# Attention in front of a routed expert layer: exponentials of phi into PSUM, masks by TensorE, casts and subtractions on other engines, and a written-out order

## The chip, the cores and the metric

One core of one Trainium2 chip runs one program. The time is device microseconds for one execution; lower is better. Of three timed runs of the kernel before, the median is 904.42 us (904.2 to 906.09).

## The reference

Two stages. Attention takes q, k, v of 8 batches, 8 heads, 576 positions and 64 columns; each head gets causal softmax attention plus a linear memory read by phi(q), and the two are mixed by a gate:

```
scores = q k^T / 8, masked above the diagonal, minus their row maximum
local  = softmax(scores) v
phi(x) = where(x > 0, x, exp(x) - 1) + 1          # = max(x,0) + exp(-max(-x,0))
mem    = (phi(q) M_prev) / (phi(q) z_prev + 1e-6)
x      = g*mem + (1-g)*local,  g = sigmoid(beta)   # 4608 tokens x 512
```

Then a routed layer: logits `x @ w_gate` are sorted over all (token, expert) pairs, each token takes the best expert that still has room (576 per expert), and expert e gives `relu(x w1[e]) w2[e]`.

## The kernel before

Everything is float32 in and out; TensorE works on float16 pairs. A float32 tile is cast to a float16 high half, the remainder is subtracted out as a low half, and products are summed over high and low parts.

**Attention** runs in 16 units (a unit is one batch and four of its heads). Per unit: SP loads k, q, v and M; casts make the high halves (`kh`, `qh`, `vh`, and `ph` of phi), subtractions the low halves (`kl`, `ql`, `vl`, `pl`, line 1043 and 1154 on GpSimd); TensorE transposes them (line 1052) and copies out of PSUM give `kT`, `qT`, `pT`. phi is three steps: a relu on ScalarE (`phr`, line 1137), an exponential in place in SBUF on ScalarE (`phe`, line 1138), and max-plus-add on VectorE (`phs`, line 1139), each over 18x64 = 1152 columns.

A first pass finds each row's maximum (`MX`): TensorE writes 128x512 blocks of scores to a PSUM bank `pb`, and VectorE reduces them. Rows of a block on the diagonal need the causal mask; line 1067 adds it while reducing, with one custom instruction per row block (512, 384, 256 or 128 columns), each followed by a reading of its accumulator (`DVE_READ_ACCUMULATOR2_ANT`). The maximum goes back into a spare row of `qM`, so that the second pass of scores comes out of TensorE with it subtracted. ScalarE takes the exponential (line 1205 a float16 `ph`; lines 1209 and 1212 a float32 copy), and VectorE (line 1210, from PSUM) or GpSimd (line 1213) subtracts to a low half `pl`.

Each head's output is accumulated by TensorE in `avo`, two PSUM tiles used in turn (the parts AV1, AV2, AV3), and the memory's part in `avm`, one tile (AVm). VectorE then makes the denominators (N0: lines 1260 for `avo`, 1261 for `avm`), their reciprocal (N1, 1265), and scales both (N2, 1264); GpSimd adds the two (`nadd`, 1272), and a cast and a subtraction give `xs`, which goes to DRAM and, transposed, to the gate's logits. In one head of four VectorE adds instead (N2b, N3: line 1278).

**Order.** Each piece of work is a node with engines it may run on, costs, dependences and buffers from pools (`pb` 5, `av` 2, `am` 1, ...). `Sched.run` is a planner: it walks simulated time with those costs and the priorities and offsets of the table `PR` (`off`, `dl`, `pin` for the engine) and emits one list; each engine executes its share of that list in order, and waits between engines are semaphores that the tile layer derives from the tiles that instructions write and read. **The expert layer** (`moe_all`) has a planner run of its own.

Of the kernel before, what the change touches and what calls it, by code (L numbers as in the profile page):

```python
# [23 lines left out]
 'dl': {'0': {'AV': -2321.92,  # L24
              'MX': 1567.76,
              'N': -24421.58,
              'P2': -4357.96,
              'S': 101.14,
              'fin1': 22868.1,
              'fin2': 10356.86,  # L30
              'kb': 10286.06,
              'kh': -45730.44,
              'kl': 20174.46,
              'kt': -4701.95,
              'lk': -12408.59,
              'lm': -8436.44,
              'lq': -2541.36,
              'lv': -3.36,
              'maxrem': 3733.37,
              'mfin': 29276.67,  # L40
              'mfin2': -10538.29,
              'mfin3': 7506.77,
              'mh': -11209.39,
              'ml': -432.1,
              'mz': 12658.92,
              'nadd': -11907.02,
              'ncast': -7225.71,
              'nsub': -10647.97,
              'ph': -1228.79,
              'phe': -9589.46,  # L50
              'phr': 524.92,
              'phs': 2230.42,
              'pl': 4308.28,
              'proc24': 3267.06,
              'pt': 11255.13,
              'qh': -4155.4,
              'ql': 7002.13,
              'qmove': -223.83,
              'qt': 10808.21,
              'sj4': 22053.16,  # L60
              'vh': -293.15,
              'vl': -4289.79},
        '1': {'AV': -11630.65,
              'MX': 5085.57,
              'N': -6291.91,
              'P2': -3722.96,
              'S': 0.29,
              'fin1': 18360.27,
              'fin2': -6498.84,
              'kb': -13149.86,  # L70
              'kh': -9834.86,
              'kl': -14831.77,
              'kt': 2765.98,
              'lk': -26.17,
              'lm': -31.5,
              'lq': -62.5,
              'lv': 65.33,
              'maxrem': 241.19,
              'mfin': 827.99,
              'mfin2': 5904.98,  # L80
              'mfin3': 8067.82,
              'mh': -6693.41,
              'ml': -3921.85,
              'mz': 12321.27,
              'nadd': 28446.8,
              'ncast': -5424.62,
              'nsub': -11693.87,
              'ph': 492.03,
              'phe': 2716.39,
              'phr': -7873.98,  # L90
              'phs': -15036.85,
              'pl': 8602.27,
              'proc24': -8298.99,
              'pt': 9687.89,
              'qh': 27462.53,
              'ql': -726.83,
              'qmove': -2093.73,
              'qt': -7770.46,
              'sj4': 1.71,
              'vh': -3758.76,  # L100
              'vl': -4489.33},
        '10': {'AV': 2861.92,
               'MX': 0.01,
               'N': -4207.12,
               'P2': -7603.6,
               'S': -0.44,
               'fin1': -11796.22,
# [36 lines left out]
               'P2': -700.32,
               'S': 0.11,
               'fin1': -8124.01,
               'fin2': -3919.93,
               'kb': 9923.63,
               'kh': 12644.97,
               'kl': -13145.41,  # L150
               'kt': -4241.87,
               'lk': -6151.58,
               'lm': -7286.77,
               'lq': 7551.39,
               'lv': 7510.93,
               'maxrem': 2.79,
               'mfin': 22015.1,
               'mfin2': 6463.64,
               'mfin3': -7945.76,
               'mh': -9010.16,  # L160
               'ml': 7934.19,
               'mz': -3520.69,
               'nadd': 2187.16,
               'ncast': 12966.79,
               'nsub': -4987.87,
               'ph': 4067.79,
               'phe': 16439.48,
               'phr': -16517.7,
               'phs': 7862.4,
               'pl': 3996.54,  # L170
               'proc24': 2350.4,
               'pt': -0.15,
               'qh': 1067.34,
               'ql': 512.84,
               'qmove': -18712.55,
               'qt': -9981.91,
               'sj4': -4091.57,
               'vh': -11967.99,
               'vl': -5668.57},
        '12': {'AV': 13431.14,  # L180
               'MX': -0.34,
               'N': 6485.25,
               'P2': -2957.52,
               'S': 0.54,
               'fin1': -4378.18,
               'fin2': 23705.86,
               'kb': -1628.06,
               'kh': -4672.12,
               'kl': 9427.26,
               'kt': -3533.86,  # L190
               'lk': -3255.11,
               'lm': 3597.42,
               'lq': 2527.1,
               'lv': 5090.06,
               'maxrem': 0.14,
               'mfin': -7530.28,
               'mfin2': -24054.29,
               'mfin3': -4992.24,
               'mh': 2100.24,
               'ml': 10776.14,  # L200
               'mz': -6507.17,
# [542 lines left out]
class Sched:  # L744
# [18 lines left out]
    def run(self,tol=100,sem=170,same=110,t0=0.0,hwg=450,dlat=1300,dend=950,ph=2800.0,thr=3060,pel=60):  # L763
# [43 lines left out]
        while left:  # L807
            b=None
# [966 lines left out]
```

## Time and profile before

| | us |
|---|---|
| timed runs, median (lowest to highest) | 904.42 (904.2 to 906.09) |
| the profiled execution, its own time | 910.64 |
| its span, first to last instruction | 908.8 |
| attention, filling: 0 to 100 of the span | 100 |
| attention, steady: 100 to 425 | 325 |
| attention, last head, last logits, routing's preparation: 425 to 441 | 16 |
| routing and experts: 441 to 908.8 | 468 |

A row of an engine gives its busy time. For TensorE a record of a matmul lasts longer than the engine is taken by it (the next starts long before the record ends), so TensorE's share is an upper bound. On VectorE and ScalarE one record's last 0.08 to 0.1 us lie under the next record's start, so the cost of an instruction in a full queue is the distance between two starts.

### The profile page before, as it was taken

The page shows a single profiled execution, that of the slowest core. Times are in us where ns is not written, and L with a number is a line of the kernel's source. Part 1 is how long each engine was busy: PE and PEld are TensorE (multiplying, and loading weights), DVE is VectorE, ACT ScalarE, POOL GpSimd, SP SyncE. Part 2 cuts the span into 40 slices and gives each one's busy share as a digit, 9 for nine tenths or more (in the row PEclk, how much of TensorE's full clock was granted, in tenths as well). Part 3 has the DMA queues.
Part 4 walks back from the last instruction along what each step waited for, and adds up shares of the span by engine and source line. Part 5 has one row for each costly group of instructions (what it writes and reads, how often), then busy time and mean ns, then how long its engine had stood idle before and what let it go on. Part 6 is the DMA issues. An engine that isn't in the chain of part 4 may idle for free.

```text
span 908.8 us, 24389 instructions
## 1 busy us (share of the span) xinstructions
PE 803.3 (88%) x9240; PEld 526.2 (58%) x9240; DVE 670.7 (74%) x2507; ACT 580.7 (64%) x1027; POOL 543.7 (60%) x564
## 2 busy tenths in 40 slices
PE   3687998999999899999226999999999999999995
PEld 2475887777787688888115445454444444444442
DVE  8798898999999899997788878787867774111020
ACT  4767787887898888976226674848383846552120
POOL 5776886887898786866104492928174646852101
PEclk9999899999999999999557999999999999999998
DMA  5566777765757566334124455566463828940001
GB/s 127 117 142 132 166 155 156 165 149 127 161 130 168 120 139 136 86 71 92 48 93 146 164 144 195 143 213 148 167 168 124 226 89 208 248 150 18 35 13 41
DMA packets 231755, 120.86 MB, mean 133 GB/s; under 512 B 199509, under 2 KB 208725, under 8 KB 231637
## 3 DMA queue, kind: packets, MB, share of 16 engines
q1 hardware_dynamic: 225749, 100.42, 45.2%
q0 software_dynamic: 5888, 18.88, 6.7%
q8 instruction: 72, 1.18, 0.5%
q14 instruction: 46, 0.38, 0.1%
HBM read 72.40 MB, written 18.87 MB: 100 GB/s over the span
## 4 chain that ended last, share of the span: by engine, by line
PE 49%; DVE 22%; issue 12%; DMA 6%; POOL 5%; ACT 3%; SPq 2%; another core or an unknown queue 0%; POOLq 0%; DVEq 0%; ACTq 0%
PE py L1417 15%; PE ph L1417 15%; PE pb L892 7%; PE avo L892 5%; DVE pb L1067 4%; DVE scr L1658 2%; DVE xt L1264 2%; DMA xT<-xs 2%; PE pb L1052 2%; PE prem L1417 2%; DVE pl L1210 2%; SPq L959 1%; POOL h L1043 1%; PE pr L1417 1%; DMA qM<-qT 1%
## 5 line engine op out<-in xcount | busy, mean ns | idle before, releaser
L1574 POOL TENSOR_TENSOR wl<-wst,wh 128x1024 f16<-128x1024 f32 x62 | 131.3, 2140 | 80.8 <-ACT wh L1573 59.5
L1417 PE MATMUL ph<-xT,wh 128*128 128x512 f16 (+1 forms) x560 | 162.9, 364 | 2.8 <-DVE hl L1617 1.4
L1067 DVE CUSTOM_DVE_ANT_0 pb<-pb,maskF 128x128 f32<-128x128 f32 (+3 forms) x256 | 124.7, 497 | 7.4 <-PE pb L892 3.7
L892 PE MATMUL pb<-qT,kT 128*128 128x64 f16 (+3 forms) x576 | 106.1, 245 | 8.2 <-DVE mx L1067 1.8
L1636 POOL DMA_INDIRECT out_dram<-ys,idx x40 | 38.9, 973 | 119.1 <-ACT ys L1631 99.8
L1205 ACT ACTIVATE ph<-pb 128x512 f16<-128x512 f32 x144 | 86.0, 597 | 29.1 <-PE pb L892 23.0
L1617 DVE SCALAR_TENSOR_TENSOR hl<-ph,hh 128x512 f16<-128x512 f32 x64 | 44.0, 688 | 80.2 <-ACT hh L1616 77.2
L1417 PEld LDWEIGHTS <-wh 128*128 128x128 f16 x1072 | 68.4, 98 | 59.6 <-issue 3.5
L892 PE MATMUL pb<-qM,kB 128*128 128x64 f16 (+3 forms) x576 | 99.2, 244 | 1.7 <-DMA qM<-mr 1.7
L1417 PE MATMUL py<-wh,hh 128*128 128x512 f16 x256 | 97.0, 379 | 1.5 <-ACT hh L1616 1.1
L1417 PE MATMUL ph<-xT,wl 128*128 128x512 f16 (+1 forms) x280 | 97.7, 363 | 0.0
L1417 PE MATMUL py<-wl,hh 128*128 128x512 f16 x256 | 97.0, 379 | 0.0
L1417 PE MATMUL prem<-xT,wh 128*128 128x64 f16 x512 | 96.3, 193 | 0.0
L1658 DVE TENSOR_SCALAR_CACHE_REDUCE scr<-p_LwT,th 128x320 f16<-128x320 f32 x168 | 85.1, 543 | 2.7
L1616 ACT ACTIVATE hh<-ph 128x512 f16<-128x512 f32 x64 | 38.0, 593 | 76.2 <-PE ph L1417 55.5
L892 PE MATMUL pb<-kT,qM 128*128 128x512 f16 (+5 forms) x384 | 77.6, 314 | 8.8 <-DVE mx L1067 3.4
L1417 PEld LDWEIGHTS <-hh 128*128 128x128 f16 x512 | 47.3, 97 | 56.2 <-ACT hh L1616 1.3
L1656 ACT ACTIVATE scs<-p_LwT,th 128x320 f16<-128x320 f32 x84 | 47.0, 560 | 50.7 <-DVE th L1665 40.2
L892 PE MATMUL avo<-V,ph 128*128 128x65 f16 x1344 | 78.7, 194 | 0.0
L892 PE MATMUL avo<-V,pl 128*128 128x65 f16 x672 | 74.9, 196 | 0.0
L892 PEld LDWEIGHTS <-ph 128*128 128x128 f16 x1344 | 70.6, 98 | 5.1 <-issue 0.9
L1496 POOL DMA_INDIRECT xg<-xd,idx x40 | 38.6, 964 | 51.6 <-DVE sa L1517 35.0
(304 smaller groups left out, 2358.3 us busy)
## 6 DMA issues: line engine op xcount, KB each, us to landing
wst<-in_moe_w_dram SPq DMA_DIRECT2D x32, 1024.0 KB, 7.7
kf<-in_k_dram SPq DMA_DIRECT2D x64, 128.0 KB, 2.8
qf<-in_q_dram SPq DMA_DIRECT2D x64, 128.0 KB, 2.8
xd<-xs SPq DMA_DIRECT2D x16, 512.0 KB, 3.5
vf<-in_v_dram SPq DMA_DIRECT2D x48, 128.0 KB, 2.8
kB<-kT SPq DMA_DIRECT2D x15, 288.0 KB, 3.4
qM<-qT SPq DMA_DIRECT2D x15, 288.0 KB, 5.5
vF<-in_v_dram SPq DMA_DIRECT2D x16, 128.0 KB, 3.1
```

Source lines behind the costliest of these rows:

```text
L892: def MM(*a,**kw): mm(*a,skip_group_check=True,**kw)
L1052: for i in range(a,b_): nc.tensor.transpose(p[:,128*(i-a):128*(i-a)+128],g()[:,i],cst['idh'])
L1067: Q=lambda o,i,n: nc.vector.tensor_tensor_reduce(out=i,in0=i,in1=cst['maskF'][:,512-n:512],scale=1.0,scalar=-3e38,op0=ALU.add,op1=ALU.max, ...
L1205: c=SC.add('Eh',[('A',478)],lambda x,a=a: nc.scalar.activation(phs_[x.buf['ph']][:,0:512],pbb[a.buf['pb']],AF.Exp,scale=0.125),acq=('ph',) ...
L1417: def MM(*a,**kw): mm(*a,skip_group_check=True,**kw)
L1496: SC.add('gather',[('P',1250 if i<4 else 1200,'p',0,(1250,'n'))],lambda x: G_.indirect_dma_start(out=xg[0:r_,i],out_offset=None,in_=xd,in_ ...
L1574: SC.add('sp',[('P',2079)],lambda x,ws=ws,k=k,s=s: G_.tensor_sub(wl[:,k,s],ws(),wh[:,k,s]),r=[key+('h',)],w=[key+('l',)],after=[b],rel=rel ...
L1616: b=SC.add('hh',[('A',478)],lambda x,a0=a0,f=f: A_.activation(hh[:,f],phb[a0.buf['ph']],AF.Relu),w=[('hh',f)],after=[y],prio=pr('hh',n,pos ...
L1617: SC.add('hl',[('V',602)],lambda x,a0=a0,f=f: V_.scalar_tensor_tensor(hl[:,f],phb[a0.buf['ph']],0.0,hh[:,f],op0=ALU.max,op1=ALU.subtract), ...
L1636: SC.add('scat',[('P',1250 if i<4 else 1200,'p',0,(1250,'n'))],lambda x,e=e,i=i,r_=r_: G_.indirect_dma_start(out=outv[5*n+i],out_offset=ba ...
L1656: SC.add('sign',[('A',547)],lambda x,j=j,t_=t_,c_=c_: A_.activation(scs[j-KV],LwT,AF.Sign,bias=t_[:,4:5],accum_out=c_[:,j:j+1]),r=['LwT',( ...
L1658: V(462,lambda x,j=j,t_=t_,c_=c_: V_.tensor_scalar(scr[j],LwT,t_[:,j+1:j+2],0.0,op0=ALU.is_ge,op1=ALU.add,accum_out=c_[:,j:j+1]),r=['LwT', ...
```

## The change

Only attention is edited; `moe_all` stands as it was.

- phi's exponential goes to a PSUM bank of the pool `pb`, in pieces of 8, 8 and 2 tiles (512, 512, 128 columns) instead of in place in SBUF; `phs` reads it there.
- The masks of the smaller row blocks (384, 256, 128 columns) are added by TensorE, as one more 128x128 matmul of `identb` with `maskM` per block, and VectorE takes plain maxima (`TENSOR_REDUCE`), two blocks of 256 in one instruction. The 512-column block keeps the custom instruction.
- `avo` and `avm` become one tile `avb` of three banks (`avo` 0, `avm`, `avo` 1), so that N0 is one instruction for both denominators and, in three heads of four, N2 one of 640 columns.
- Beyond the first unit, low halves (`kl`, `ql`, `vl`, `pl`, `p4s`, `ml`, `nsub`) run on GpSimd alone; the high-half casts and the relu no longer have VectorE as a choice; copies of the memory (`mz`, `mh`, `mh2`) run on ScalarE alone.
- The planner is not run for attention: `Sched.given` takes a list of node numbers, of chosen engines and of buffers (`PR_ORDER`), which replaces the tables `dl`, `off` and `pin`.

```diff
-              'phe': -9589.46,
+ 'dl': {},
+ 'off': {},
+ 'pin': {},
+PR_ORDER = ('''
+5 24 3 21 26 4 22 25 1 23 2 27 28 31 0 32 41 29 43 42 30 45 6 44 47 245 46 49 239 57 111 51 48 241 50 59 238 114 53 115 440 61 52 58 116 242 63 9 60 112 243 62 10 65 8 64 67 7 70 240 66 14 69 68
...
+    def given(self,ids,alts,bufs):
+
+        al,bu=[iter(''.join(x.split())) for x in (alts,bufs)]; free={k:set(range(v)) for k,v in self.pools.items()}; out=[]
+        for i in map(int,ids.split()):
+            x=self.n[i]; a=x.alts[int(next(al)) if len(x.alts)>1 else 0]; x.eng=a[0]; x.var=a[2] if len(a)>2 else None
+            assert all(d.start is not None for d in x.deps)
+            for p in x.acq: x.buf[p]=int(next(bu)); free[p].remove(x.buf[p])
+            for p,o in x.rel: free[p].add(o.buf[p])
+            x.start=len(out); out.append(x)
...
-    avo=[ps.tile([128,512],F32,name=f'avo{i}') for i in range(2)]; avm=ps.tile([128,512],F32,name='avm')
+    avb=ps.tile([128,3,512],F32,name='avb'); avo=[avb[:,0],avb[:,2]]; avm=avb[:,1]
...
+            rq=MK(u)+[('qMz',u%3)]; mk=lambda o: MM(o,identb,maskM,start=False,stop=True)
...
-                        MM(p[:,0:384],qT[:,4*h+2],kq(h,3),start=True,stop=True)
-                        MM(p[:,384:512],qT[:,4*h],kq(h,1),start=True,stop=True)
-                    def f2(p,h=h): Q(mx[:,4*h+2:4*h+3],p[:,0:384],384); Q(mx[:,4*h:4*h+1],p[:,384:512],128)
+                        MM(p[:,0:384],qT[:,4*h+2],kq(h,3),start=True,stop=False); mk(p[:,256:384])
+                        MM(p[:,384:512],qT[:,4*h],kq(h,1),start=True,stop=False); mk(p[:,384:512])
+                    def f2(p,h=h): R(mx[:,4*h+2:4*h+3],p[:,0:384]); R(mx[:,4*h:4*h+1],p[:,384:512])
...
-                    for y in range(2): Q(mx[:,8*h2+4*y+1:8*h2+4*y+2],p[:,256*y:256*y+256],256)
+                def f2(p,h2=h2): R(mx[:,8*h2+1:8*h2+8:4],p.rearrange('p (a b) -> p a b',b=256))
...
-            SC.add('phe',[('A',Ac(n))],lambda x,a=a,b_=b_,UE=u%NE: nc.scalar.activation(ef[UE][:,a:b_],ef[UE][:,a:b_],AF.Exp,scale=-1.0),w=K('ef',u%NE,a,b_),prio=pr('phe',u))
+            for c0_ in range(a,b_,8):
+                c1_=min(c0_+8,b_); n=n64(c0_,c1_); pv=lambda x,n=n: pbb[x.buf['pb']][:,0:n].rearrange('p (t d) -> p t d',d=64)
+                y=SC.add('phe',[('A',75+.81*n)],lambda x,a=c0_,b_=c1_,UE=u%NE,pv=pv: nc.scalar.activation(pv(x),ef[UE][:,a:b_],AF.Exp,scale=-1.0),r=K('ef',u%NE,c0_,c1_),acq=('pb',),prio=pr('phe',u))
+                SC.add('phs',[('V',Vt(n))],lambda x,a=c0_,b_=c1_,U2=U2,UE=u%NE,pv=pv,y=y: nc.vector.scalar_tensor_tensor(ef[UE][:,a:b_],qf[U2][:,a:b_],0.0,pv(y),op0=ALU.max,op1=ALU.add),r=K('qf',U2,c0_,c1_),w=K('ef',u%NE,c0_,c1_),after=[y],rel=[('pb',y)],prio=pr('phs',u))
...
-        SC.add('mz',al('mz',u,a=97,v=75),lambda x,u=u,U2=U2: cp(x.var,mf[U2][:,:,64],zT[0:64,4*u:4*u+4]),r=['zT'],w=[('mf',U2,2)],prio=pr('mz',u))
+        SC.add('mz',al('mz',u,a=90),lambda x,u=u,U2=U2: cp(x.var,mf[U2][:,:,64],zT[0:64,4*u:4*u+4]),r=['zT'],w=[('mf',U2,2)],prio=pr('mz',u))
...
-                nc.vector.scalar_tensor_tensor(de[:,0:5],own(0,5)[:,:,64],1.0/256,eg(0,5),op0=ALU.mult,op1=ALU.add)
-                nc.vector.scalar_tensor_tensor(de[:,5:10],mem()[:,:,64],1.0/256,eg(5,10),op0=ALU.mult,op1=ALU.add)
+            def f(x): nc.vector.scalar_tensor_tensor(des[di],both()[:,:,:,64],1.0/256,eps[:,g,5*bo():5*bo()+10].rearrange('p (k i) -> p k i',i=5),op0=ALU.mult,op1=ALU.add)
...
-    order=SC.run(**P_.get('run',{}))
+    order=SC.run(PR_ORDER)
```

What each engine executes differs at two places that matter below.

VectorE before, in the maxima of one unit and the scaling of one head (`ISA pb,mx<-pb,maskF` is the custom maximum, `ISA mx` its reading, `xt` the scaled output N2):

```order
L1067 ISA pb_180,mx_162<-pb_180,maskF 128x384
L1067 ISA mx_162 128x1
L1067 ISA pb_180,mx_162<-pb_180,maskF 128x128
L1067 ISA mx_162 128x1
L1264 TENSOR_TENSOR xt_170<-avo_104,de_166 128x320
L1264 TENSOR_TENSOR xt_170<-avm,de_166 128x320
```

VectorE now, at such a place (`de` are the denominators, N0 and N1; `ef` is phi's sum, read from a `pb` bank):

```order
L678 SCALAR_TENSOR_TENSOR de_165<-avb,eps 128x10
L682 RECIPROCAL de_165<-de_165 128x10
L480 TENSOR_REDUCE mx_161<-pb_179 128x1 x2
L687 TENSOR_TENSOR xt_167<-avb,de_165 128x640
L480 TENSOR_REDUCE mx_161<-pb_177 128x2
L625 TENSOR_TENSOR pl_140<-pb_178,ph_133 128x512
L480 TENSOR_REDUCE mx_161<-pb_179 128x1 x2
L554 SCALAR_TENSOR_TENSOR ef_111<-qf_108,pb_177 128x512
```

The pairs of custom maxima with their readings became plain reductions without a reading, N0 and N2 one instruction each, and phi's sum three shorter ones.

TensorE before, where the memory's part of one head (`avm`) ends and the next head's accumulation (`avo`) starts; what an instruction waits for stands in brackets:

```order
L892 MATMUL avm<-ml_131,pT_125 128x65
L892 LDWEIGHTS pT_125
L892 MATMUL avm<-mh_129,pT_125 128x65
L892 LDWEIGHTS pT_125
L892 MATMUL avm<-ml_131,pT_125 128x65
L892 MATMUL avo_105<-vF_159,pf_150 128x65 x2
L892 MATMUL avo_105<-vF_159,pf_151 128x65
L892 LDWEIGHTS qM_99
```

TensorE now, inside one head's accumulation (the end of AV1 and the start of AV2, both into bank 0 of `avb`):

```order
L306 MATMUL avb<-V_103,ph_131 128x65
L306 LDWEIGHTS pl_138 [waits Pool_49]
L306 MATMUL avb<-V_103,pl_138 128x65
L306 LDWEIGHTS ph_134
L306 MATMUL avb<-V_103,ph_134 128x65 [waits DVE_49]
L306 LDWEIGHTS ph_134
L306 MATMUL avb<-V_103,ph_134 128x65
```

And VectorE now, the instructions of the head before that this accumulation waits for, one for each of AV1, AV2 and AV3 (N2, N2b, N3; they read bank 1, bank 2 and bank 2):

```order
L682 RECIPROCAL de_165<-de_165 128x10
L681 TENSOR_TENSOR xt_166<-avb,de_165 128x320
L681 TENSOR_TENSOR avb<-avb,de_165 128x5x64
L695 TENSOR_TENSOR xt_166<-avb,xt_166 128x320
L348 CAST xs_170<-xt_166 128x5x64
```

Matmuls into these banks that wait for VectorE were 22 in the whole program and are 111. Followed back to the instruction that each waits for, 109 of them wait for one that reads other banks than the matmul writes: the waits go by the tile, and the three banks are one tile now.

## Rows read from the trace of the kernel before

**Rows 1.** Stretches: us, busy us of PE, PEld, DVE, ACT, POOL, clock, DMA:
```profile
0.00:100.00 100.00, 69.45 (x920) 52.57 (x920) 83.81 (x259) 65.01 (x110) 67.59 (x143) 0.95 0.63 138
100.00:425.00 325.00, 307.76 (x5354) 258.71 (x5351) 305.87 (x998) 273.24 (x497) 260.11 (x272) 0.99 0.60 133
425.00:441.00 16.00, 9.66 (x168) 8.76 (x164) 8.76 (x42) 4.68 (x10) 7.06 (x9) 0.78 0.45 117
441.00:909.00 468.00, 416.44 (x2810) 206.11 (x2810) 272.30 (x1210) 237.75 (x412) 208.92 (x143) 0.94 0.45 133
```
**Rows 2.** Who waited for whom, 100 to 425: total us, times, longest:
```profile
ACT ph L1205 <- PE pb L892: 22.5, 22, 3.6
POOL xt L1272 <- DVE xt L1264: 10.2, 6, 4.1
```
**Rows 3.** The same view, 0 to 441, TensorE on VectorE's scaling:
```profile
PE avm L892 <- DVE xt L1264: 1.3, 1, 1.3
```
**Rows 4.** Timeline, TensorE: start us, length us, instruction:
```profile
251.23 0.19 PE L892 MATMUL avm<-ml,pT 128*128 128x65 f16 x1
251.26 0.38 PE L892 MATMUL pb<-qT,kT 128*128 128x512 f16 x1
251.48 0.38 PE L892 MATMUL pb<-qM,kB 128*128 128x512 f16 x1
251.69 0.22 PE L892 MATMUL pb<-maskT,identb 128*128 128x128 bf16 x1
...
255.42 0.22 PE L892 MATMUL pb<-qM,kB 128*128 128x128 f16 x1
255.47 0.22 PE L892 MATMUL pb<-maskT,identb 128*128 128x128 bf16 x1
```
**Rows 5.** Timeline, VectorE:
```profile
251.29 0.16 DVE L1260 SCALAR_TENSOR_TENSOR de<-avo,eps 128x5 f32<-128x5 f32 x1
...
252.27 0.54 DVE L1067 CUSTOM_DVE_ANT_0 pb<-pb,maskF 128x384 f32<-128x384 f32 x1
252.73 0.14 DVE L1067 DVE_READ_ACCUMULATOR2_ANT mx<- 128x1 f32 x1
252.91 0.30 DVE L1067 CUSTOM_DVE_ANT_0 pb<-pb,maskF 128x128 f32<-128x128 f32 x1
253.12 0.14 DVE L1067 DVE_READ_ACCUMULATOR2_ANT mx<- 128x1 f32 x1
253.12 0.48 DVE L1264 TENSOR_TENSOR xt<-avo,de 128x320 f32<-128x320 f32 x1
253.53 0.48 DVE L1264 TENSOR_TENSOR xt<-avm,de 128x320 f32<-128x320 f32 x1
253.92 1.28 DVE L1210 TENSOR_TENSOR pl<-pb,ph 128x512 f16<-128x512 f32 x2
255.12 0.42 DVE L1067 CUSTOM_DVE_ANT_0 pb<-pb,maskF 128x256 f32<-128x256 f32 x1
...
255.98 0.69 DVE L1066 TENSOR_REDUCE mx<-pb 128x1 f32<-128x512 f32 x1
256.58 0.29 DVE L1066 TENSOR_REDUCE pb<-pb 128x2 f32<-128x128 f32 x1
```
**Rows 6.** Groups on VectorE, 0 to 441: busy us, mean ns, idle before:
```profile
L1139 DVE SCALAR_TENSOR_TENSOR ef<-qf,ef 128x1152 f32<-128x1152 f32 x15 | 20.6, 1371 | 0.0
L934 DVE CAST p<-ef 128x1152 f16<-128x1152 f32 x15 | 14.1, 940 | 0.0
L934 DVE COPY mf<-zT 64x4 f32<-64x4 f32 x15 | 11.7, 778 | 0.0
```
**Rows 7.** Groups on GpSimd, the same stretch:
```profile
L1213 POOL TENSOR_TENSOR pl<-pf,ph 128x512 f16<-128x512 f32 x49 | 59.6, 1217 | 10.3 <-ACT pf L1212 8.2 <-issue 1.8
L935 POOL TENSOR_SCALAR h<-qf 128x640 f16<-128x640 f32 x1 | 0.7, 722 | 2.5 <-DMA qf<-in_q_dram 2.5
```
**Rows 8.** Timeline, GpSimd:
```profile
258.17 1.91 POOL L1213 TENSOR_TENSOR pl<-pf,ph 128x512 f16<-128x512 f32 x1 [0.49 <-ACT pf L1212]
```

More of the change, by code (lines that the diff above doesn't have):

```diff
@@ L762, in add, with run @@
         self.n.append(x); return x
-    def run(self,tol=100,sem=170,same=110,t0=0.0,hwg=450,dlat=1300,dend=950,ph=2800.0,thr=3060,pel=60):
+    def given(self,ids,alts,bufs):
[6 more added lines that the diff above has]
+            x.start=len(out); out.append(x)
+        assert len(out)==len(self.n)
+        return out
+    def run(self,order=None,tol=100,sem=170,same=110,t0=0.0,hwg=450,dlat=1300,dend=950,ph=2800.0,thr=3060,pel=60):
+        if order: return self.given(*order)
         N=len(self.n)
@@ L988, in f @@
         for y in vf: nc.gpsimd.memset(y[64:128,RB:NVT:2],0.0); nc.gpsimd.memset(y[0:64,RB+1:NVT:2],0.0)
-    one('avz',[('P',3000)],f,-150,w=['avz']+[('vf',i,x_) for i in range(2) for x_ in range(RB,NVT)])
+    one('avz',[('P',4300)],f,-150,w=['avz']+[('vf',i,x_) for i in range(2) for x_ in range(RB,NVT)])
     one('bt',dq(23),lambda x: nc.sync.dma_start(out=bt,in_=bass.AP(tensor=beta.tensor,offset=beta.offset,ap=[[0,128],[1,8]])),-188,w=['bt'])
@@ L996, in f @@
         V_.reciprocal(gt,gt);
-        for i in range(10): V_.tensor_scalar(eps[:,:,i],gt[:,:,i//5],(1e-9,1e-6)[i//5]/256,None,op0=ALU.mult)
-    one('gt',[('V',700)],f,-155,r=['bt'],w=['gt'])
+        for i in range(15): V_.tensor_scalar(eps[:,:,i],gt[:,:,i//5%2],(1e-9,1e-6,1e-9)[i//5]/256,None,op0=ALU.mult)
+    one('gt',[('V',1670)],f,-155,r=['bt'],w=['gt'])
     for i in range(2):
@@ L1006, in f @@
             put(129,g0); nc.gpsimd.tensor_sub(cl4[i][:,0:NHd],g0[:,0:NHd],V16[i][:,0:RB,129].rearrange('p (h t) -> p h t',t=4)[:,:,0]); put(64,cl4[i])
-        one('put',[('P',1150)],f,-154+20*i,r=['gt'],w=[('V16g',i)])
+        one('put',[('P',1900)],f,-154+20*i,r=['gt'],w=[('V16g',i)])
     for i in range(NVF):
@@ L1100, in f @@
                     for y in range(2): MM(p[64*y:64*y+64],qT[:,16+h2,64*y:64*y+64],kq(2*h2+y,4),start=True,stop=True)
[L1101 removed]
+                part('MX',f,lambda p,h2=h2: R(mx[:,16+h2:17+h2],p),1024,220,598,[('qM',u%3,16+h2)]+kk,(h2,3),x0+5)
             for gi,G in enumerate(gs):
@@ L1204, in scores @@
                         ch('E',c); B_.append((c,)); continue
-                    c=SC.add('Eh',[('A',478)],lambda x,a=a: nc.scalar.activation(phs_[x.buf['ph']][:,0:512],pbb[a.buf['pb']],AF.Exp,scale=0.125),acq=('ph',),after=[a]+ch('E'),prio=pr('S',u,3*j+w+P_.get('eoff',0)))
+                    c=SC.add('Eh',[('A',486)],lambda x,a=a: nc.scalar.activation(phs_[x.buf['ph']][:,0:512],pbb[a.buf['pb']],AF.Exp,scale=0.125),acq=('ph',),after=[a],prio=pr('S',u,3*j+w+P_.get('eoff',0)))
                     ch('E',c)
@@ L1207, in scores @@
                     if (UO(u).get('p2k') or P_['p2k'])[3*j+w]=='v':
-                        d=SC.add('Ef',[('A',478)],lambda x,a=a: nc.scalar.activation(pbb[a.buf['pb']],pbb[a.buf['pb']],AF.Exp,scale=0.125),after=[a,c],prio=pr('S',u,3*j+w+P_.get('eoff',0)))
+                        d=SC.add('Ef',[('A',490)],lag=-110,fn=lambda x,a=a: nc.scalar.activation(pbb[a.buf['pb']],pbb[a.buf['pb']],AF.Exp,scale=0.125),after=[a,c],prio=pr('S',u,3*j+w+P_.get('eoff',0)))
                         e=SC.add('P2v',[('V',602)],lambda x,a=a,c=c: nc.vector.tensor_sub(pls_[c.buf['ph']][:,0:512],pbb[a.buf['pb']],phs_[c.buf['ph']][:,0:512]),after=[c,d],rel=[('pb',a)],prio=pr('P2',u,3*j+w))
```

770 lines of the change are left out of this document (41 added, 729 removed), and 84 rows, old and new, of the table PR_ORDER.

## The prediction

> **What bounds the kernel now.** I read the stretches first: routing and experts (441 to 909) are not edited, so the 441 us of attention are what can move [rows 1]. Adding its three stretches, VectorE is busy 398.5 us of 441 (90%, and 94% from 100 to 425), ScalarE 342.9, GpSimd 334.8. TensorE's record says 387, but that is too much: the last `avm` matmul starts 0.03 before the next instruction and is recorded for 0.19, and one of 512 columns holds the engine 0.22 with a record of 0.38 [rows 4]. The program's order counts 737,456 columns in attention (a float32 column as four); at 0.22 per 512 that is 317 us, 72%. Next the waits: ScalarE waits 22.5 us for scores, GpSimd 10.2 for VectorE's scaling [rows 2], while the big VectorE groups have almost no idle time before them [rows 6]. So VectorE sets the pace of the steady stretch, with the three others 12 to 20% below it. The sum below is therefore one of loads: what the busiest engine has to do, and how much of the 441 us it manages to fill (now 398.5/441 = 0.90).
>
> **VectorE's load.** Costs are distances between starts, counts are those of the program's two orders.
>
> Blocks of 384 and 128 columns: 64 pairs, each 252.27 to 253.12 = 0.85 us, of which the two instructions take 0.46 and 0.21 and one reading 0.18 [rows 5]. Plain reductions have no reading; taken at the pace of the custom ones, 0.67. 64 x 0.18 = -11.5 (if as fast as the 512-column reduction, 0.60: -16; if each is 0.08 slower: -1).
>
> Blocks of 256: 32 pairs, 255.12 to 255.98 = 0.86, become one reduction of 512 columns, 255.98 to 256.58 = 0.60 [rows 5]: -8.3.
>
> N0 loses 64 instructions of 0.16 at most, N2 48 that shared 0.80 a pair [rows 5]; what goes is the fixed part alone, since the columns stay. Bounds 0 and 112 x 0.16 = -18; I take 0.07 each, -8, near the 0.08 that the records overlap by.
>
> phi's cast (15 of 0.94) and the copy `mf<-zT` (15 of 0.78) leave VectorE [rows 6]; less the 0.08 overlapped each, -12.9 and -10.5. The copy has four columns: it is dear because it waits.
>
> phi's sum: 15 of 1.37, less overlap 19.4, against 16 times 0.60 + 0.60 + 0.21 by the pace of the reductions, 22.6; the first unit's old pieces give 1.5 back: +2.
>
> Moved by the list: ten more casts of 320 columns (0.41 each, as N2's) and six of `mr`, 17 copies of 256 columns fewer: +2.
>
> Sum -47, from 398.5 to 351. Bounds: -30 to -62.
>
> **The other engines.** TensorE: 192 mask matmuls of 128 columns, 0.055 each as the mask at 255.47 starts that long after the matmul before it [rows 4]: +10.6, to 328. Nothing hides them on TensorE; at 74% of 441 they do not bind.
>
> ScalarE: eleven casts of phi and 15 small copies more, 13 wide casts and 29 of 320 columns fewer, copies out of PSUM in both directions: 3,300 columns fewer of some 343 us, so within 5 us of before, say 340.
>
> GpSimd: 18 wide casts (19,392 columns) and 19 of 320 come over. The only such cast in the trace takes 0.72 for 640 columns [rows 7], so 25,472 columns cost 28.7. Against that, GpSimd's subtraction at 258.17 took 1.91 where the mean is 1.22 [rows 7, 8]: VectorE was then in phi's old sum over two SBUF tiles. If each of 15 such sums cost it half a microsecond, 7 go: 335 + 22 = 357, at most 364.
>
> The Trainium skill (SBUF — State Buffer, Who interferes with whom) says that a VectorE instruction with two SBUF inputs, or a copy in a two-port mode, and a GpSimd instruction that reads SBUF block each other for the whole of whichever came first. The trace agrees in the 1.91 and in the 0.78 of a four-column copy. By that rule every one of the 15 sums could cost GpSimd its whole length, 19 us by the group's row, and GpSimd would come out at 345; the sum here stays at 357.
>
> phi's pieces take 48 more turns of the five `pb` banks. At some 1.3 us each (two instructions of 0.6 and the handing over) that is 62 of 2,205 bank-microseconds; I cost it at nothing, and if the cover fails it shows as TensorE waiting for a bank.
>
> **The wait that is added.** Now 109 accumulation matmuls wait for N0, N2 or N3 of the head before, though these read other banks. In the trace TensorE waited for that scaling once, 1.3 us [rows 3]. The last `avm` matmul starts at 251.23, N0 at 251.29, N2's second half ends about 253.92 [rows 4, 5]: 2.7 us in which a head's result is still being read. Behind a waiting matmul stands all of TensorE's queue, scores and transposes too, and ScalarE waits for those. Bounds: 0, if TensorE has that much other work in between, and 63 changes of head x 2.7 = 170. In the order, TensorE's columns between a head's end and the waiting matmul come to 0 to 2 us for N0 and mostly 1.2 to 4.8 for the scalings; VectorE's queue up to the awaited instruction, at the distances above with 0.6 for two handovers, is longer than that by 25 us summed over the 93 waits I can follow. This lies nearer the low row. I count it not as load but as lost filling.
>
> The Trainium skill (PSUM — Partial Sum Buffer, PSUM bank collisions raise a hardware error) asks for a guard by bank, not by address or tile; by that rule none of the 109 waits is needed. It changes what one would write next, and the sum only in that a wait of this kind need not be there.
>
> **The sum.** The busiest engine falls from 398.5 to 357. With four engines between 328 and 357 none waits for one alone, and 25 us of new waits come in, so the filling should fall below 0.90; at 0.90 attention would take 395, at 0.80 446. I take 0.845: 422.5, which is -18.5. Against the profiled execution, 910.64 - 18.5 = 892.1; the median of the runs is 0.9932 of that execution, so 886.
>
> **Rivals.**
>
> *All of it arrives* (0.14): filling stays 0.90, 357/0.90 = 395, -46, 859 on the median's scale. For: VectorE's near-absent idle time, and load falls on each queue that waits for it. Against: 83.8 of the first 100 us, where transfers and first casts bound, hardly shrink [rows 1].
>
> *GpSimd becomes the bound, or the plain reductions are no quicker* (0.15): GpSimd at 364 with filling 0.83 gives 438.5, or VectorE at 371 (without the first two terms) with 0.845 gives 439; -2, 902, and with a little less 898. For: GpSimd's share now is 80% in the steady stretch and it gets the casts. Against: it waits for others now [rows 2] and its work has slack until the transposes.
>
> *The cross-bank waits decide* (0.21): slower. TensorE needs 328 plus W. It can fill about 0.94 of a stretch in which it is the bound (its recorded share of the steady one), so it decides once 328 + W passes 0.94 x 441 = 415, W = 87, or 1.4 us at each of 63 changes of head. At 1.5 us W is 95, attention 423/0.94 = 450, +9, 913 on the median's scale. For: two waits per change in the order, some with nothing between, and a chain of 2.7 us. Against: the waited-for instructions mostly stand early enough in VectorE's queue, and VectorE now has time for them.
>
> **How the numbers follow.** The forecast, 872 to 897, has 0.50. A median can be told from no change at about 0.2%, 1.8 us. Faster: 0.50 + 0.14 + half of the second rival, 0.08 = 0.72; same: the rest of it, 0.07; slower: 0.21. The range leaves out half of the first rival's 0.14 below and most of the third's end above: 862 to 911, with the predicted time that of the likeliest case, 886.
>
> **What would show it.** The experts' stretch keeps 468 us. Right: VectorE's load in attention near 351 and its share of the steady stretch under 88%; no reading after a reduction; the group of 256-column pairs gone and 512-column reductions at 0.60 between starts; `mf<-zT` on ScalarE under 0.2; GpSimd's load about 357, with `pl` subtractions near 1.16. Right on the waits: TensorE waiting for `xt` and `de` some tens of times with a sum of 10 to 30 us. Wrong: that sum above 80; GpSimd's idle time gone; VectorE still above 370; attention ending after 441, or before 400.

## The result, and the profile after

The changed kernel takes 913.53 us in the median of 7 runs (909.81 to 918.48), against 906.17 for the kernel before (7 runs): a ratio of 1.0081, 95% interval [1.0053, 1.0109]. It is slower by some 7 us, where 886 was forecast. The profiled execution of after took 909.81 us, the shortest of its seven, and that of before 910.64, 4.5 us above its median, so the two traces lie some 8 us closer together than the medians do.

The stretches of after (us, busy us of PE, PEld, DVE, ACT, POOL, clock, DMA share), to be read beside [rows 1]:

```profile
0.00:100.00 100.00, 81.04 (x1188) 63.73 (x1189) 84.89 (x222) 82.00 (x152) 79.75 (x158) 1.00 0.62 139
100.00:425.00 325.00, 302.75 (x5301) 256.10 (x5298) 268.43 (x699) 261.49 (x493) 266.38 (x293) 0.99 0.61 131
425.00:441.00 16.00, 10.88 (x141) 9.71 (x137) 6.31 (x20) 1.43 (x3) 6.50 (x9) 0.70 0.44 131
441.00:909.00 468.00, 416.20 (x2814) 206.94 (x2814) 274.84 (x1228) 237.34 (x412) 209.85 (x143) 0.94 0.45 133
```

VectorE's load came down as meant, from 398.4 to 359.6 us of 441. But attention ends no earlier: the last head's reciprocal (N1) starts at 432.1 us before and at 434.6 after, with 476.7 and 473.4 us of the program behind it. The head start is there (the first unit is through at 65.4 us, before at 77.7), and it is given back: from the second unit's end to the fifteenth's it is 313.5 us before and 324.3 after, and the last unit takes 18.2 us instead of 10.6.

The groups of after in attention (busy us, mean ns, then the idle time before them and what ended it) show that the edits did what they say. To be read beside [rows 6, 7]:

```profile
L480 DVE TENSOR_REDUCE mx<-pb 128x1 f32<-128x384 f32 x64 | 35.1, 549 | 4.2 <-PE pb L306 3.7 <-PE pb L466 0.3
L480 DVE TENSOR_REDUCE mx<-pb 128x2 f32<-128x512 f32 x32 | 21.9, 686 | 4.2 <-PE pb L306 4.2
L687 DVE TENSOR_TENSOR xt<-avb,de 128x640 f32<-128x640 f32 x48 | 39.4, 821 | 10.6 <-PE avb L306 6.3 <-POOL xs L697 1.4 <-POOL jp L786 0.7
L554 DVE SCALAR_TENSOR_TENSOR ef<-qf,pb 128x512 f32<-128x512 f32 x32 | 21.4, 681 | 1.0 <-ACT pb L553 0.9
L678 DVE SCALAR_TENSOR_TENSOR de<-avb,eps 128x10 f32<-128x10 f32 x64 | 10.5, 163 | 15.6 <-PE avb L306 15.5
L628 POOL TENSOR_TENSOR pl<-pf,ph 128x512 f16<-128x512 f32 x49 | 56.8, 1158 | 7.6 <-ACT pf L627 7.4
L347 ACT COPY mf<-zT 64x4 f32<-64x4 f32 x16 | 3.1, 191 | 0.0
```

What is new stands at the right: VectorE, which had almost no idle time before, waits for TensorE's accumulators, and TensorE waits for VectorE. TensorE's waits of after, 0 to 441 us (total us, times, longest), against one of 1.3 us in [rows 3]:

```profile
PE avb L306 <- DVE xt L687: 11.5, 18, 1.4
PE avb L306 <- DVE xt L695: 2.4, 5, 0.6
PE avb L306 <- DVE xt L681: 2.2, 4, 0.6
PE avb L306 <- DVE avb L681: 2.0, 4, 0.6
```

VectorE's waits for the accumulators, before and then after:

```profile
DVE de L1260 <- PE avo L892: 4.2, 3, 2.9
DVE de L1261 <- PE avm L892: 1.3, 3, 0.7
```

```profile
DVE de L678 <- PE avb L306: 15.5, 24, 3.2
DVE xt L687 <- PE avb L306: 6.3, 10, 1.8
DVE xt L695 <- PE avb L306: 4.5, 8, 0.9
DVE avb L681 <- PE avb L306: 4.4, 6, 0.9
DVE xt L681 <- PE avb L306: 3.0, 6, 0.8
```

So the one tile makes waits in both directions, and the prediction counted only TensorE's: VectorE's grew from 5.5 to 33.7 us. N0 has always waited for its own head's sums. Behind N0 nothing of the own head is outstanding, so the 18.2 us in front of N2, N2b and N3 (the last four rows) are waits for matmuls into banks that these instructions do not read; before has none there.

The last unit shows one wait of each direction (start us, length us, instruction, in brackets the idle time before it and its releaser). TensorE:

```profile
427.48 0.19 PE L306 MATMUL avb<-ml,pT 128*128 128x65 f16 x1
427.51 0.86 PE L306 MATMUL avb<-vF,pf 128*128 128x65 f32 x6
429.81 3.57 PE L306 MATMUL avb<-vF,pf 128*128 128x65 f32 x22 [1.44 <-DVE xt L687]
433.18 0.63 PE L306 MATMUL avb<-vF,p4f 128*128 128x65 f32 x2
```

and VectorE beside it:

```profile
428.41 0.17 DVE L678 SCALAR_TENSOR_TENSOR de<-avb,eps 128x10 f32<-128x10 f32 x1 [1.09 <-PE avb L306]
428.61 0.22 DVE L682 RECIPROCAL de<-de 128x10 f32<-128x10 f32 x1
428.93 0.82 DVE L687 TENSOR_TENSOR xt<-avb,de 128x640 f32<-128x640 f32 x1
```

Six matmul records of the last head go into one bank; the others stand until N2 has read the head before, 0.06 us behind its end at 429.75. They write the bank that N2 does not read. TensorE has nothing else left to do here. N0 in its turn had waited for the six, 0.04 us behind their end, though it reads only the two banks of the head before.

### The profile page after: what moved, and what is told of

It is laid out like the page before. It is cut to its first block, busy times and chain, and to the rows that moved or that the text cites. A ratio compares the mean times of both kernels' runs of the same rounds, so it can differ in the third digit from the quotient of the medians.

```text
span 908.0 us, 24573 instructions
## 1 busy us (share of the span) xinstructions
PE 810.9 (89%) x9432; PEld 536.5 (59%) x9432; DVE 634.5 (70%) x2169; ACT 582.3 (64%) x1059; POOL 562.5 (62%) x602
## 4 chain that ended last, share of the span: by engine, by line
PE 38%; issue 9%; DVE 6%; POOL 1%; DMA 1%; ACT 1%; POOLq 0%; DVEq 0%
PE py L834 16%; PE ph L834 14%; PE avb L306 3%; PE prem L834 2%; DVE scr L1075 2%; DMA wst<-in_moe_w_dram 1%; PE pb L306 1%; POOL out_dram L1053 1%; PE pr L834 1%; PE pl L834 1%; DVE xt L687 1%; DVE th L1082 0%; ACT wh L990 0%; DVE kk L1081 0%; ACT wst L989 0%
## 5 line engine op out<-in xcount | busy, mean ns | idle before, releaser
L306 PE MATMUL pb<-qT,kT 128*128 128x64 f16 (+3 forms) x576 | 103.4, 243 | 1.3 <-DVE pl L625 0.9
L306 PE MATMUL pb<-qM,kB 128*128 128x64 f16 (+3 forms) x576 | 97.2, 241 | 0.5 <-DMA qM<-mr 0.4
L480 DVE TENSOR_REDUCE mx<-pb 128x1 f32<-128x384 f32 (+3 forms) x192 | 89.6, 504 | 9.8 <-PE pb L306 9.2
L306 PE MATMUL avb<-V,ph 128*128 128x65 f16 x1344 | 77.8, 193 | 13.6 <-DVE xt L687 7.2
L306 PE MATMUL pb<-kT,qM 128*128 128x512 f16 (+5 forms) x384 | 81.2, 310 | 5.8 <-DMA qM<-qT 3.0
L306 PE MATMUL avb<-V,pl 128*128 128x65 f16 x672 | 74.4, 196 | 0.0
```

What stands on the lines that cost most here:

```text
L306: def MM(*a,**kw): mm(*a,skip_group_check=True,**kw)
L480: R=lambda o,i: nc.vector.tensor_reduce(o,i,axis=mybir.AxisListType.X,op=ALU.max)
```

## Experiments

Each ran in five rounds; ratios are to runs of the kernel before on the same chip, with a 95% interval, and a difference between two kernels is that of their ratios, in us of 906. "Ends" is the start of the last N1 in the profiled execution, by which attention can be compared (before 432.1, after 434.6). The runs were made on several chips, and the unedited part behind the last N1 takes 472 to 484 us in their traces, so ends compare to a few us only, and the ratios decide.

**a1_split**: after, with three tiles.

```
-avb=ps.tile([128,3,512],F32,name='avb'); avo=[avb[:,0],avb[:,2]]; avm=avb[:,1]
+avo=[ps.tile([128,512],F32,name=f'avo{i}') for i in range(2)]; avm=ps.tile([128,512],F32,name='avm')
 (N0, N2: one instruction for avo, one for avm)
```

> The kernel after, in its order, with the three accumulator banks as three PSUM tiles again; N0 and N2 are therefore two instructions each. 44 instead of 111 accumulator matmuls wait on VectorE. Theory W (waits on a bank that is not written, 20.7 us of TensorE's idle time from 100 to 400 us, ate the gain): most of these 20.7 us come back in attention, less some 8 us of VectorE's load that returns off the path, so 893 to 902 against 913 for the kernel after. Theory O (the new order decides: the engines wait for each other along a list that was fixed beforehand, and a wait removed in one place returns in another): within 4 us of the kernel after, 909 to 917, with TensorE's waits for scores or transposes larger by what those for the accumulators lose. Theory P (TensorE with 328 us and its waits sets the pace): as W, but only as much as TensorE's waits fall.

Measured 0.9916 [0.9884, 0.9948], ends 416.8. Against after that is 1.65%, 15 us (with both intervals about 11 to 19), although VectorE issues 112 instructions more: theory W. VectorE's waits for the accumulators fall with TensorE's, from 33.7 to 6.9 us (3.9 and 3.0 in front of N0), so the 15 us are the price of both directions together. It is also faster than before by 0.8%. The last unit takes 11.4 us instead of 18.2, since TensorE now works on under the scaling. TensorE, then VectorE, in the last unit:

```profile
410.87 0.23 PE L306 MATMUL avo<-V,ph 128*128 128x65 f16 x2
...
411.58 0.19 PE L306 MATMUL avo<-V,pl 128*128 128x65 f16 x1
```

```profile
410.60 0.15 DVE L679 SCALAR_TENSOR_TENSOR de<-avo,eps 128x5 f32<-128x5 f32 x1
...
411.18 0.49 DVE L683 TENSOR_TENSOR xt<-avm,de 128x320 f32<-128x320 f32 x1
411.59 0.49 DVE L683 TENSOR_TENSOR avo<-avo,de 128x320 f32<-128x320 f32 x1
```

**b1_onetile**: before, with the one-tile line of the diff above and nothing else.

> The kernel before with its order and all instructions unchanged; only its three accumulator banks are one PSUM tile, so that 99 instead of 22 accumulator matmuls wait on VectorE. Theory W: the waits cost 10 to 25 us here too, 916 to 931. Theory O: the old order was not made for these waits, and they cost at least as much as W says; but then the kernel after without them (a1_split) does not gain them back. If both are wrong and such waits are covered: within 3 us of 906.

Measured 1.0414 [1.0385, 1.0443], ends 468.8: 38 us, far more than expected. The waits that the profile shows (0 to 470 us) are no longer than in after:

```profile
PE avb L892 <- DVE xt L1264: 11.2, 19, 1.0
PE avb L892 <- DVE de L1261: 3.4, 10, 0.5
PE avb L892 <- DVE avb L1264: 1.7, 3, 1.2
PE avb L892 <- DVE xt L1278: 1.1, 2, 0.6
```

These are 17.4 us. VectorE's waits for the accumulators are 39.8 us (5.5 in before), the two largest of them:

```profile
DVE de L1260 <- PE avb L892: 20.3, 19, 6.6
DVE xt L1264 <- PE avb L892: 15.8, 21, 1.4
```

So the waits of both directions have about the size that they have in after (18.1 and 33.7), and cost 38 us here against 15 there. Why, no run shows. Two readings fit: VectorE has 393 us of load up to the last N1 of before, in after 356, so there is less room for its waits; and what stands behind TensorE's wait (scores, which ScalarE waits for, whose exponentials VectorE waits for) comes late as well, while the new list may have been made with these waits in it.

**a9_avopair**: a1_split with the two `avo` banks as one tile and `avm` as its own.

> a1_split with the two banks of the scores' accumulators as one tile and the memory's accumulator as its own: 124 instead of 44 accumulator matmuls wait on VectorE, now only for readers of the other avo bank. It splits the 16 us of the waits. If those on avo make them (the next head's first accumulation behind the scaling of the head before): 10 to 16 us slower than a1_split. If those between avo and avm do: within 4 us of it.

Measured 1.0002 [0.9972, 1.0032], ends 433.3: 8 us slower than a1_split (with both intervals 4 to 12). It lies between the two sizes: the waits within the `avo` pair make about half of the 15 us. That the rest comes from those between `avo` and `avm` was not run by itself. TensorE's waits for VectorE at the pair are 9.5 us here, half of after's, and VectorE's for the accumulators 33.8, as in after.

**a2_custom** and **b2_masks**: the smaller maxima alone, on the old instruction in after, on the new one in before.

```
-MM(p[:,0:384],...,stop=True)                  f2: Q(...,384); Q(...,128)
+MM(p[:,0:384],...,stop=False); mk(p[:,256:384])  f2: R(...); R(...)      (b2; a2 the other way)
```

> The kernel after with the smaller maxima (384, 128 and 256 columns) on VectorE's custom instruction again: 192 mask matmuls fewer on TensorE (-10.6 us of it by 0.055 each), some 20 us more on VectorE. Theory P (TensorE sets the pace): 3 to 10 us faster than after, 903 to 910. The load sum of the prediction (the busiest engine decides; VectorE 359 to 379): 10 to 24 us slower, 923 to 937. Theory O: within 4 us.

> The kernel before, in its order, with the smaller maxima as plain reductions and their masks on TensorE: 20 us less on VectorE, 10.6 more on TensorE. The load sum (VectorE's 398 sets the pace): 10 to 20 us faster, 886 to 896. Theory P: 3 to 10 slower, 909 to 916. Theory O: within 4 us of 906.

Measured 1.0126 [1.0099, 1.0153] for a2, 4 us above after, and 1.0028 [1.0009, 1.0047] for b2, 2.5 above before. The load sum fails at b2: VectorE gives up some 13 us by its starts (398 to 385) and the kernel is slower.

**b3_pe** and **b4_nomask** take b2 apart.

```
b3: +zk=lambda o: MM(o,identb,cst['maskF'][:,0:128],start=False,stop=True)  (in mk's places; f2 stays Q)
b4:  f2: R instead of Q, no mk
```

> The kernel before with 192 matmuls of 128 columns more (they add zeros behind the products of the smaller maxima): TensorE +10.6 us, VectorE unchanged. It prices TensorE's load alone. If TensorE's own time sets the pace one for one: +8 to +12 us, 912 to 916. If VectorE does, as the load sum of the prediction has it: within 3 us of 904. b2_masks, which has the same matmuls and 14 us less on VectorE, came out at +2.5.

> The kernel before with the smaller maxima as plain reductions and no masks at all (left out: the causal mask in the row maxima of the 384, 128 and 256 column blocks): VectorE some 14 us less by its starts in b2_masks, TensorE unchanged. It prices VectorE's load alone. Load sum (VectorE sets the pace): -12 to -18 us, 886 to 892. If TensorE with its waits sets the pace: 0 to -4, 900 to 904. If both share it: about -8, the b2_masks result less what b3_pe adds.

Measured 1.0037 [1.0016, 1.0057] and 0.9972 [0.9952, 0.9992]: 10.6 us more on TensorE cost 3.4, 13.5 less on VectorE gave 2.5. Neither engine sets the pace alone, and VectorE's microsecond is worth about 0.2 (0.05 to 0.3 by the interval).

**a5_nomask, d1_dve, d2_pool, d3_act**: the same question in a1_split, one engine at a time.

```
d1: -nc.vector.tensor_sub(pls_[..][:,0:512],...)   +nc.vector.tensor_sub(pls_[..][:,0:256],...)   (u>0)
d2: the same on nc.gpsimd; d3: phr, p's and V's cast over half the columns; a5: as b4
```

> a1_split without the masks of the smaller maxima (left out as in b4_nomask): TensorE -10.6 us, VectorE unchanged, in the new order. If TensorE sets the pace there: -8 to -11 against a1_split (895), 884 to 887. If no single engine does: 0 to -5.

> a1_split with VectorE's subtraction for the low halves over 256 of its 512 columns from the second unit on (left out: the rest of these low halves, which stay stale): 89 instructions shorter by some 0.28 us, -25 us of VectorE and nothing else. If VectorE sets the pace: 868 to 874. At the price that b4_nomask showed (0.18 of a us per us): 889 to 893.

> a1_split with GpSimd's subtraction for the low halves over 256 of its 512 columns from the second unit on (left out as in d1_dve): 46 instructions shorter by some 0.55 us, -25 us of GpSimd. If GpSimd sets the pace: 868 to 874. If no engine does alone: 885 to 893.

> a1_split with ScalarE's wide instructions of phi and V over half their columns (left out: half of 15 relus of phi, of 10 casts of phi and of 7 casts of V, which stay stale): some 0.5 us less each, -16 us of ScalarE. If ScalarE sets the pace: 878 to 881. If no engine does alone: 887 to 893.

Measured 0.9854 [0.983, 0.9878] for a5 (-5.6 us against a1_split), 0.9869 [0.9842, 0.9895] for d1 (-4.3), 0.9867 [0.9841, 0.9893] for d2 (-4.4), 0.9896 [0.9867, 0.9926] for d3 (-1.8; its interval and those of d1 and d2 overlap with a1_split's). They end at 414.6, 415.2, 416.3 and 415.0. GpSimd's load fell by 21.8 us by its starts (354 to 332), and attention ended half a microsecond earlier. With both intervals a microsecond of VectorE, GpSimd or ScalarE is worth between nothing and about 0.4, and one of TensorE in a5 0.2 to 0.8: a price of one is excluded for each.

**d5_pe** and **b5_pe**: TensorE 30 us shorter, in a1_split and in before.

```
-MM(o,l,ml[:,h],start=False,stop=True)
-MM(o,ph,vv[:,0:65],start=False,stop=False)
```

> a1_split without the accumulator matmuls of V's low half (720 of them) and of the memory's low half (320): left out, so the accumulators lose these halves. At 0.029 and 0.030 us between starts TensorE loses 30 us, no other engine anything. Theory P (once the first unit is through, TensorE sets the pace: 359 us of 417 by its own starts, not the 328 of the prediction): -18 to -30 us against a1_split, 865 to 877. If the engines' order and latencies decide, as for VectorE and GpSimd (25 us less gave 4): -3 to -8, 887 to 892.

> The kernel before without the same 1040 matmuls: TensorE -30 us. Theory P holds there more weakly (352 of 432 us by its starts): -8 to -20, 886 to 898 on a scale where before has 906. If VectorE set the pace there, as the prediction had it: within 3 us of before.

Measured 0.9807 [0.9784, 0.983] (-10 us, ends 411.8) and 0.9975 [0.9955, 0.9995] (-2). My theory P falls: a third of the 30 us arrives in the new order, a twelfth in the old. The waits say where about half of the rest went: 11 us more stand in front of two transfers and a subtraction. TensorE's waits, a1_split, then d5_pe (0 to 441 us):

```profile
PE pb L306 <- DMA qM<-qT: 6.0, 5, 2.0
PE pb L306 <- DMA xT<-xs: 5.3, 2, 3.2
```

```profile
PE pb L306 <- DMA qM<-qT: 9.4, 5, 2.9
PE pb L306 <- DMA xT<-xs: 9.0, 5, 4.0
PE pb L306 <- DVE pl L625: 4.1, 5, 2.8
```

**d4_all**: the edits of a5, d1, d2 and d3 together.

> a1_split with the reductions of a5_nomask, d1_dve, d2_pool and d3_act together (left out as there): TensorE -11, VectorE -18, GpSimd -22, ScalarE -13 us. If the single gains add: -5.6, -4.3, -4.4 and -1.8 make -16, a ratio of 0.974 to before. Theory P: as TensorE falls, the others being off its path, -6 to -10, 0.981 to 0.985. If all four set the pace together by equal shares: -15 to -20 or more, 0.97 or less.

Measured 0.9822 [0.9795, 0.985], ends 412.9: 8.5 us for some 64 us of load on four engines. That is less than the 16 of the single runs together, though their intervals, some 13 us on that sum, do not exclude it.

**a6_phsb, c1_edits, c2_order**: phi's exponentials, and the order apart from the edits.

```
a6: -phe ... out=pbb[x.buf['pb']], acq=('pb',)        +phe ... out=ef[UE][:,a:b_]
c1: before + b2's edit + MV={'kh':'**apaa...','qh':...,'ph':...,'vh':...,'mz':'aaa...','ncast':...}  (x.var from after)
c2: a6 + a2's edit + cp('v',...) for phi's cast and mf
```

> a1_split with phi's exponentials written back into SBUF in place, in the same order: 48 turns of the pb banks fewer, VectorE's 48 sums with both inputs in SBUF. If the bank turns cost nothing, as the prediction had it, and the sum over two SBUF tiles hinders GpSimd: within 3 us of a1_split or up to 8 slower (GpSimd's subtractions longer, mean of pl above 1.2). If the bank turns cost: 2 to 8 us faster than a1_split, 887 to 893.

> The old order with new instructions: before with the plain reductions and their masks on TensorE (as b2_masks), and with the casts of k, q, V, phi and the scaled rows and the copy of zT on the engines that after has for them, each at its old place in the list; phi's exponentials stay in SBUF and the accumulators in three tiles, as in a6_phsb. VectorE loses some 37 us, GpSimd gains some 25. The load sum: 875 to 890. If the gain of such edits needs an order made for them: within 6 us of 906, while a6_phsb, which has the same instructions in the new order, stood at 1.001 and c2_order (old instructions in the new order) at 1.028.

> The new order with the old instructions, as far as it can hold them: a1_split with the custom maxima and no masks, phi's exponentials in SBUF, and phi's whole cast and the copy of zT on VectorE again. If the new order by itself is what makes a1_split faster than before: 892 to 900. If the edits make it, each at the price that the runs so far show (custom +4, phi in SBUF +9, 23 us more on VectorE at 0.18 each +4): 908 to 916, so that the new order alone is no better than the old one.

Measured 1.001 [0.9988, 1.0032], 1.0139 [1.0115, 1.0163] and 1.0283 [1.0254, 1.0312]. The old list with old instructions stands at 1, with new ones at 1.014; the new list with old instructions at 1.028, with new ones (a6) at 1.001. Each list is best with the instructions it was made for (c2 holds the old ones as far as the new list can), and the pairing alone is worth 1 to 3%. a1_split is 8.5 us ahead of a6_phsb, but that too is an instruction exchanged in a list made for the other one: in a6 25 of the 32 sums of 512 columns start while a GpSimd instruction is under way, in before 1 of 15 sums does. What that costs stands in the last section. No run gives the gain of phi's move to PSUM by itself.

**a8_lglate**: a1_split with eleven groups of logits some 50 places later in the list.

> a1_split with its list changed in one respect: eleven of the sixteen groups of routing logits stand some 50 places later in the list, so that the transposing transfer they wait for (xT) has landed before TensorE comes to them; nothing else is moved but what waits for them, and pb banks where one is taken. In a1_split TensorE waited 5.3 us for these transfers and 5.9 us stood in front of the logits. If what holds the kernel is such waits in TensorE's fixed list: 3 to 6 us faster than a1_split, a ratio to before of 0.985 to 0.988. If the wait returns in front of the next instruction (scores that wait for ScalarE or for qM): within 2 us of it.

Measured 0.9925 [0.9892, 0.9958], ends 424.6: nothing gained (with both intervals between 3 us faster and 5 slower than a1_split). The waits for `xT` are gone, and these came up (a1_split, then a8_lglate, 0 to 441 us; the first rows of a1_split's waits on transfers stand above):

```profile
ACT ph L620 <- PE pb L306: 18.6, 28, 1.8
```

```profile
ACT ph L620 <- PE pb L306: 25.4, 29, 3.6
PE pb L306 <- DMA qM<-qT: 9.8, 6, 2.3
```

a1_split thus remains the version that beats both kernels, by 0.8% before and 1.6% after.

## Why the prediction was wrong

*The loads.* VectorE was forecast at 351 us and has 359.6; GpSimd at 357 and has 352.6; ScalarE at 340 and has 344.9 (sums of the first three stretches). Reductions came as forecast: 0.60 between starts for the pairs of 256, no reading, 0.47 and 0.20 for 384 and 128 columns. N0 and N2 gained 0.06 us an instruction, near the 0.07 forecast: the fused N2 takes 0.74 between starts, the two halves 0.80. The copy of `zT` takes 0.19 on ScalarE, and GpSimd's subtraction fell from 1217 to 1158 ns, near the 1.16 us forecast. TensorE's 10.6 us for the masks held (11 by starts in b3_pe). But its level did not: I dismissed the recorded 387 us and took 317 from the columns. By the median distance between starts of each form the matmuls need 352 us before and 359 after, so it was never idle to a quarter. The count had float32 too cheap. The 240 float32 matmuls of 65 columns stand in the trace of before as 480 records (busy us, mean ns, idle before):

```profile
L892 PE MATMUL avo<-vF,pf 128*128 128x65 f32 x448 | 57.0, 275 | 0.8 <-DVE de L1261 0.5 <-DVE xt L1278 0.3
L892 PE MATMUL avo<-vF,p4f 128*128 128x65 f32 x32 | 6.2, 275 | 0.0
```

Their starts lie 0.112 us apart in the median, 54 us in all, where four times the columns at 0.22 per 512 are 27. The rest is short float16 matmuls, 0.029 to 0.034 between starts for 65 columns instead of 0.028.

*The wait.* 18.1 us of TensorE's waits in four rows, 25 forecast; a1_split puts the price of all waits of the one tile at 15 us. Mechanism and size hold for this direction; the other one, VectorE's 28 us more of waiting for TensorE, is not in the prediction. The prediction's 0.6 us for two handovers stands in no row: in the last unit one engine starts 0.06 and 0.04 us behind the other's end. The rival that they decide named 913 and the kernel took 913.5, but not by its working: that asked for 95 us of waits. The Trainium skill (PSUM — Partial Sum Buffer, PSUM bank collisions raise a hardware error) has the guard go by bank. a1_split follows it, with the banks guarded one by one, and is 1.65% faster than after; what happens to banks without any guard, no run here shows.

*phi's bank turns* at nothing held: TensorE waits 1.3 us in all of after for a bank that phi's sum has to release (two rows, 1.1 and 0.2). a6_phsb has no such turns and is 8.5 us slower, but for another reason (last section).

*The step that failed* is the sum: "the busiest engine falls from 398.5 to 357" divided by a filling, 0.90 or 0.845. It charges every microsecond taken off VectorE at more than one. Instead the filling fell with the load: up to the last N1 VectorE fills 0.91 before (393.4 of 432.1 us) and 0.82 after (356.3 of 434.6). The runs price VectorE's microsecond at 0.2 (b4_nomask, d1_dve), GpSimd's at 0.2, ScalarE's at 0.14, TensorE's at 0.1 to 0.5. And where the prediction expected the gain, in the steady stretch, there is none, even without the waits. From the second unit's end to the fifteenth's, before and then a1_split (us, busy us of PE, PEld, DVE, ACT, POOL, clock, DMA):

```profile
108.06:421.55 313.49, 296.35 (x5145) 248.39 (x5142) 295.07 (x965) 263.86 (x480) 249.99 (x261) 0.99 0.61 134
```

```profile
89.75:405.47 315.72, 303.06 (x5290) 259.98 (x5288) 270.81 (x793) 263.78 (x499) 267.43 (x293) 0.97 0.64 139
```

VectorE has 24 us less to do there and the stretch is 2 us longer, with 17 us more on GpSimd, 7 more on TensorE's record and a slightly lower clock. All that a1_split gains lies ahead of it: its second unit ends at 89.8 us instead of 108.1, in the filling that the prediction took to "hardly shrink". Which edit shortens the filling was not run. By the ratio the gain is 7.6 us (the two traces have 15), and the 15 us of waits turn it into a loss of 7.

The chain of waits, which I did not use, already spoke against a sum over VectorE alone. Its largest shares from 65 to 412 us, before and then a1_split:

```profile
by line: PE pb L892 17.9%; PE avo L892 10.6%; DVE pb L1067 8.9%; issue 6.4%; DMA xT<-xs 5.8%; DVE xt L1264 4.8%; DVE pl L1210 4.5%; PE pb L1052 4.0%; SPq L959 3.1%; DMA qM<-qT 2.6%; POOL h L1043 2.0%; DVE mx L1067 1.9%; PE avm L892 1.9%; DV
```

```profile
by line: PE pb L306 31.6%; PE avo L306 22.9%; PE pb L466 7.2%; DMA xT<-xs 4.4%; DMA qM<-qT 4.2%; PE avm L306 4.0%; issue 3.2%; DMA qM<-qM 1.9%; DVE pl L625 1.8%; DVE mx L480 1.7%; DVE xt L683 1.2%; SPq L373 1.2%; DMA qf<-in_q_dram 1.1%; ACT
```

Summed over all lines, VectorE, busy for 94% of the steady stretch, stands on 32% of the chain in before, TensorE on 35%: most of VectorE's load lay beside work that was as late. In a1_split it is 8%, and TensorE has 66%. The shares are no prices: the runs have 0.2 where the chain has 0.32 (b4_nomask) and 0.3 where it has 0.66 (d5_pe).

The signs that the prediction named for being right nearly all came true (VectorE's share of the steady stretch 83%, GpSimd's load, the waits of TensorE at 18 us), and the kernel is slower: none of them tested the step from load to time.

*Left open.* What sets the pace without the waits. No single engine's load sets it one for one, since 64 us on four engines brought 8.5, and the one wait that was removed (a8_lglate) came back elsewhere. That it is the fixed list with the latencies of its transfers and hand-overs fits c1, c2 and the waits of d5_pe, but was not shown: no run had another list made for a1_split's instructions. The prices, too, come from lists that stayed as they were; what a microsecond is worth when the list is made anew was not run.

## What to carry to other kernels

Where several engines are 75 to 95% busy on fixed lists, price a microsecond by runs that remove a few, not by the busiest engine's load over its filling: here it was worth 0.1 to 0.5. An edit that joins buffers so that one instruction can read several is paid for by every writer that now waits for a neighbour's reader and by every reader that waits for a neighbour's writer; count these waits in both directions, and look first at the last unit, where nothing covers them. Instructions and their list belong together: changing either alone cost 1 to 3%.

## What the runs showed of the hardware

VectorE's sum for phi over 512 columns takes 681 ns with one input in PSUM; with both in SBUF (a6_phsb) it takes 1296 in the mean:

```profile
L555 DVE SCALAR_TENSOR_TENSOR ef<-qf,ef 128x512 f32<-128x512 f32 x32 | 41.0, 1296 | 0.9 <-ACT ef L554 0.8
```

The mean hides two cases. The 7 sums that start while no GpSimd instruction is under way take 673 to 693 ns, as with PSUM; the 25 others take 775 ns to 5.1 us. One of these, and GpSimd beside it (start us, length us):

```profile
313.81 1.65 DVE L555 SCALAR_TENSOR_TENSOR ef<-qf,ef 128x512 f32<-128x512 f32 x1
```

```profile
313.75 1.16 POOL L458 TENSOR_TENSOR h<-kf,h 128x512 f16<-128x512 f32 x1
```

The sum ends 0.55 us behind GpSimd's instruction, that is, it did its work behind it. The Trainium skill (SBUF — State Buffer, Who interferes with whom) says that a VectorE instruction with two SBUF inputs and a GpSimd one that reads SBUF contend; the trace agrees. Which side pays goes by which came first: in before, where 14 of the 15 sums start beside an idle GpSimd, they take 1371 ns for 1152 columns, and it is GpSimd's instruction that is longer (1.91 us in [rows 8]). In a6_phsb VectorE pays most, 26 us of load by the two groups of this sum. I had looked for the price in GpSimd's subtraction, which is at 1180 ns there and 1161 in a1_split; spread over all of its instructions GpSimd pays some 10 us too (360.8 us up to the last N1, 350.5 in a1_split).
